# First chunk: x ahead of the weights, TensorE transposes and zero matmuls; last chunk: products grouped by tile

## The chip, the cores and the metric

The kernel runs on one core of a Trainium2 chip. The metric is the device time of one execution in microseconds (us). The profile's span is about 4 us shorter than the time of the same execution (2132.2 against 2136.0 for the traced run of the kernel before), so spans are compared with spans and times with times.

## The reference, cut to what matters

A Conformer block on x of shape (2, 4000, 512) in bfloat16:

```python
h = _layernorm(x); h = _silu(h @ w_ff1_a) @ w_ff1_b; x1 = x + 0.5 * h      # first feed-forward
h = _layernorm(x1); q, k, v = h @ w_q, h @ w_k, h @ w_v                     # attention over 4000 tokens
x2 = x1 + softmax(q k^T * scale) v @ w_o
...                                            # gated convolution with a batch norm over all tokens -> x3
h = _layernorm(x3); h = _silu(h @ w_ff2_a) @ w_ff2_b; x4 = x3 + 0.5 * h     # second feed-forward
return _layernorm(x4)
```

The change touches only the first 500 of the 8000 tokens in the first feed-forward and the last 500 in the second one.

## The kernel before

The tokens go in 16 chunks of 500, four tiles of 125 each. A helper records every instruction and its buffers and emits the waits, so nearly all matmuls have one source line. The start of the program, the feed-forward and the last layer norm (cuts marked):

```python
def load_x(self, c):
    if c == 0:
        for ti in range(TPC):       # four loads of 125 rows
            self.load(self.XT[ti], self.x_flat[ti * TILE:(ti + 1) * TILE, :], [self.bx[ti]])
    ...
# program
self.load_x(0)                      # sync queue
for k in range(self.NWA):           # 16 weight loads, ACT queue
    self.load_wa(i["w_ff1_a"], k, "ACT")
    self.load_wb(i["w_ff1_b"], 2 * k, 2 * k + 2, "ACT")
self.load_x(1)
...
for ti in range(TPC):               # first chunk: normalise, then transpose by DMA
    self.ln_norm(0, 0, ti, self.ltm[ti][0:TILE, :], self.b_ltm[ti], "DVE")
    self.transpose(self.lnT[0][:, ti], self.ltm[ti], [self.b_ltm[ti]], [self.b_lnT[0][ti]])

def weights():                      # emitted at the ninth step of the first chunk
    for n, name in (("q", "w_q"), ("k", "w_k"), ("v", "w_v")):
        self.transpose(self.wst[n][0], i[name], [], [self.wst[n][1]])
    self.load(self.wst["o"][0], ...w_o...)
    self.after(6, self.fold_weights)   # products w_q w_k^T ("M") and w_v w_o, amid the first chunk

def ff_chunk(self, c, old, hook, done):
    for f in range(FC):             # 16 blocks: 4 matmuls, Silu on ACT; some steps later 4 more, one per tile
        ...
        def second(f=f, s=s):
            for ti in range(TPC):
                self.mm(self.Yb[ti][0:TILE, :], self.P[s][:, ti * TILE:(ti + 1) * TILE], self.Wb[:, f, :], ...)
            if f == FC - 1:
                for ti in range(TPC):
                    self.residual(...)
                done()              # layer norm of all four tiles together, then the stores

# out_job: in the last chunk each tile is stored by itself
ev = self.S.dma("SP", k, lambda e: e.dma_start(dst[:, lo:ti + 1, :], self.osb[o][:, lo:ti + 1, :]),
                reads=self.b_osb[o][lo:ti + 1], writes=[self.b_out[c]])   # one record for all four
```

Of the kernel before, what the change touches and what calls it, by code (L numbers as in the profile page):

```python
# [52 lines left out]
class Sync:  # L53
# [105 lines left out]
    def dma(self, e, dkey, fn, reads=(), writes=()):  # L159
        req = self._required(reads, writes)  # L160
        prev = self.count[dkey]
        if prev > 0:
            v = req.get(dkey)
            if v is None or v.val < prev:
                req[dkey] = Ev(dkey, prev, {})
        self._emit_waits(e, req)
        ins = fn(self.eng[e])
        self.count[dkey] += 16
        ins.then_inc(self.sem[dkey], 16)
        ev = Ev(dkey, self.count[dkey], dict(self.clock[e]))  # L170
        self._bind(ev, reads, writes)
        return ev
# [46 lines left out]
class Conformer:  # L219
    LN_SLOTS = 4  # L220
    NP = 8

# [12 lines left out]
    def memory(self):  # L235
# [69 lines left out]
        self.b_P = [C.buf("P", oP + s * 1024, 1000) for s in range(self.NP)]  # L305
        self.ahi = C.view(oHL, CHUNK)
# [39 lines left out]
        self.h2c = C.view(oQ1, TPC * D).rearrange("p (t d) -> p t d", t=TPC)  # L346

# [55 lines left out]
        self.b_out = [Buf("out%d" % c) for c in range(NCK)]  # L403
# [51 lines left out]

    def act(self, out, in_, func, reads, writes, **kw):
        return self.S.op("ACT", lambda e: e.activation(out, in_, func, **kw), reads=reads, writes=writes)  # L457

    def load(self, dst, src, writes, eng="SP", reads=()):
        k = self.S.dsems[self.nxt("ld", 12)]  # L460
        return self.S.dma(eng, k, lambda e: e.dma_start(dst, src), reads=reads, writes=writes)  # L461

    def transpose(self, dst, src, reads, writes):
        k = self.S.dsems[12 + self.nxt("tr", 16)]
        return self.S.dma("SP", k, lambda e: e.dma_start_transpose(dst, src), reads=reads, writes=writes)  # L465

# [4 lines left out]
    def load_x(self, c):  # L471
        if c == 0:
            for ti in range(TPC):
                self.load(self.XT[ti], self.x_flat[ti * TILE:(ti + 1) * TILE, :], [self.bx[ti]])
# [89 lines left out]

    def ff_chunk(self, c, old, hook, done):

        pops = {0: old // 2, 1: old - old // 2, 2: 0, 3: 0, 7: 2, 11: 2}
        for f in range(FC):
            ps, b_ps = self.sbank()
            s = self.nxt("P", self.NP)  # L570
            out = ps[:, 0:CHUNK].rearrange("p (t k) -> p t k", t=TPC)
            for cc in range(DC):
                self.mm(out, self.Wa[:, cc, f * 128:(f + 1) * 128], self.lnT[c % 2][:, :, cc, 0:TILE],
                        cc == 0, cc == DC - 1, [self.b_Wa[f * self.NWA // FC]] + self.b_lnT[c % 2], b_ps)
            self.act(self.P[s], ps[:, 0:CHUNK], AF.Silu, [b_ps], [self.b_P[s]])

            def second(f=f, s=s):
                for ti in range(TPC):
                    self.mm(self.Yb[ti][0:TILE, :], self.P[s][:, ti * TILE:(ti + 1) * TILE],
                            self.Wb[:, f, :], f == 0, f == FC - 1, [self.b_Wb[f], self.b_P[s]],  # L580
                            self.b_Y[ti], inc=f == FC - 1 or ti == TPC - 1)
# [8 lines left out]
            self.tick()  # L590

# [271 lines left out]
    def out_job(self, c, at, gap=1):  # L863
        sl = self.nxt("ln", self.LN_SLOTS)
        o = c % 3
        last = c == NCK - 1
        t = at
        for ti in range(TPC):
            self.after(t, lambda ti=ti: self.ln_stats(c, sl, ti))
            if ti % 2:  # L870
                t += gap
        self.after(t, lambda: self.ln_aggr(c, sl))
        t += 2 * gap

        def tile(ti):
            self.ln_norm(c, sl, ti, self.osb[o][:, ti, :], self.b_osb[o][ti], "DVE")
            dst = self.out_flat[c * CHUNK:(c + 1) * CHUNK, :].rearrange("(t p) d -> p t d", p=TILE)
            lo = ti if last else 0
            if last or ti == TPC - 1:
                k = self.S.dsems[28 + self.nxt("od", 8)]  # L880
                ev = self.S.dma("SP", k, lambda e: e.dma_start(dst[:, lo:ti + 1, :], self.osb[o][:, lo:ti + 1, :]),
                                reads=self.b_osb[o][lo:ti + 1], writes=[self.b_out[c]])
                self.out_evs.append(ev)

        for ti in range(TPC):
            self.after(t, lambda ti=ti: tile(ti))
            if ti % 2:
                t += gap
# [33 lines left out]
    def constants(self):  # L922
        S = self.S
        S.op("POOL", lambda e: e.memset(self.neghalf, -0.5), writes=[self.b_neghalf])
        for j in range(TPC):
            S.op("DVE", lambda e, j=j: e.memset(self.ltm[j], 0.0), writes=[self.b_ltm[j]])
        S.op("POOL", lambda e: e.memset(self.ident, 0.0), writes=[self.b_ident])
# [8 lines left out]
        S.op("POOL", lambda e: e.memset(self.onef, 1.0), writes=[self.b_onef])  # L936
# [8 lines left out]
    def program(self, any_score):  # L945
# [7 lines left out]
        for k in range(self.NWA):  # L953
            self.load_wa(i["w_ff1_a"], k, "ACT")
            self.load_wb(i["w_ff1_b"], 2 * k, 2 * k + 2, "ACT")
        self.load_x(1)
        if not any_score:
            self.constants()

        for ti in range(TPC):  # L960
# [3 lines left out]
        for ti in range(TPC):  # L964
            self.ln_norm(0, 0, ti, self.ltm[ti][0:TILE, :], self.b_ltm[ti], "DVE")
            self.transpose(self.lnT[0][:, ti], self.ltm[ti], [self.b_ltm[ti]], [self.b_lnT[0][ti]])
# [112 lines left out]
        def ff2(c, old):  # L1079
# [10 lines left out]
            self.ff_chunk(c, old, hook, lambda: self.out_job(c, 5 if c < NCK - 1 else 0, 1 if c < NCK - 1 else 0))  # L1090

        for c in range(NCK):
            ff2(c, len(self.lags) if c else 0)
        self.drain()
# [56 lines left out]
```

## Time and profile before

| what | value | from |
|---|---|---|
| time | 2134.14 us median of 3 (2133.32 to 2136.76) | runs |
| span of the traced run | 2132.2 us | page |
| TensorE busy | 2058.9 us, 97% | page |
| first real matmul | 28.79 us | timeline |
| second weight product (w_v w_o) starts | 56.55 us | timeline |
| last matmul to the end | 17.6 us | timeline |

A digit in a row of slices is a busy share in tenths; "<-" in a timeline or a table of waits names what ended the wait. PE is TensorE, DVE the vector engine, ACT the scalar engine, POOL GpSimd, SP the sync engine; SPq and ACTq are the queues in which SP and ACT issue DMA transfers. PSUM is the memory into which TensorE writes. The second weight product is listed as a mark: everything after it keeps its order, so the time at which it starts tells what a change to the start is worth. In the trace before:

```profile
56.55 1.03 PE L453 MATMUL s<-keys 128*128 128x512 bf16 x4
```

### The profile page before, as it was taken

To read this page: it belongs to the slowest core of one execution; us is meant where nothing else is said; L and a number is where in the kernel's file an instruction comes from. 1 tells how busy PE (TensorE), PEld (TensorE's weight loads), DVE (VectorE), ACT (ScalarE), POOL (GpSimd) and SP (SyncE) were. 2 spreads that over 40 slices of the span, in tenths; PEclk is the share of its full clock that TensorE was granted. 3 is DMA by queue.
4 is the path that set the end of the run, shared out by engine and by line. 5 is a ranking of instruction groups with operands and counts; after the bars stand their busy time and mean duration, and the time that the engine had idled before them with its cause. 6 is when DMAs were issued, how large, how long until landed. Compare 5 with 4: busy or idle time off the path is not lost.

```text
span 2132.2 us, 24365 instructions
## 1 busy us (share of the span) xinstructions
PE 2058.9 (97%) x9674; PEld 1038.7 (49%) x9674; DVE 1090.5 (51%) x2229; ACT 732.7 (34%) x1248; POOL 122.9 (6%) x257
## 2 busy tenths in 40 slices
PE   4999999999999999999999999999987999999996
PEld 2555555554444444444444444444444555555553
DVE  2444433335555666656665666566745434444442
ACT  1433333333333333333333333333324433443332
POOL 0111100000000000000000000000000000000000
PEclk9999999999999999999999999999999999999998
DMA  7122222110000000004300000000233011111110
GB/s 177 34 56 59 59 60 59 49 49 11 11 5 13 18 15 20 8 18 114 80 10 18 15 18 13 15 18 16 59 107 99 21 38 35 35 30 40 40 38 23
DMA packets 199327, 85.39 MB, mean 40 GB/s; under 512 B 147873, under 2 KB 198692, under 8 KB 199204
## 3 DMA queue, kind: packets, MB, share of 16 engines
q1 hardware_dynamic: 186468, 75.35, 14.6%
q10 hardware_dynamic: 12736, 8.39, 1.5%
q8 instruction: 78, 1.28, 0.3%
q14 instruction: 45, 0.37, 0.1%
HBM read 29.53 MB, written 19.04 MB: 23 GB/s over the span
## 4 chain that ended last, share of the span: by engine, by line
PE 93%; DVE 3%; issue 1%; DMA 1%; ACT 0%; SPq 0%; POOL 0%; ACTq 0%; POOLq 0%; DVEq 0%
PE s L453 53%; PE y L453 39%; DVE work L711 1%; DVE work L716 1%; DVE work L673 0%; DMA xt<-in_x_dram 0%; ACT work L457 0%; DVE work L491 0%; SPq L465 0%; DMA work<-work 0%; DVE work L715 0%; DVE work L514 0%; POOL work L501 0%; DVE xt L560 0%; ACTq L461 0%
## 5 line engine op out<-in xcount | busy, mean ns | idle before, releaser
L457 ACT ACTIVATE work<-s 128x500 bf16<-128x500 f32 (+1 forms) x1068 | 626.8, 587 | 1266.6 <-PE s L453 1262.0
L453 PE MATMUL s<-work,wff 128*128 128x500 bf16 x2560 | 634.3, 378 | 32.2 <-DMA work<-work 28.8
L453 PE MATMUL y<-work,keys 128*128 128x500 bf16 x2048 | 519.1, 374 | 1.3
L453 PE MATMUL s<-work,keys 128*128 128x500 bf16 x2048 | 517.5, 374 | 0.1
L453 PE MATMUL y<-wff,work 128*125 128x512 bf16 x2048 | 514.8, 379 | 0.0
L673 DVE TENSOR_TENSOR work<-work 128x500 f32<-128x500 f32 x496 | 334.8, 675 | 304.6 <-ACT work L457 302.9
L453 PEld LDWEIGHTS s<-work,wff 128*128 128x128 bf16 x2560 | 251.1, 98 | 313.3 <-issue 33.7
L453 PEld LDWEIGHTS y<-wff,work 128*125 128x125 bf16 x2048 | 279.6, 137 | 176.4
L453 PEld LDWEIGHTS y<-work,keys 128*128 128x128 bf16 x2048 | 198.0, 97 | 244.4 <-DVE work L711 15.6
L453 PEld LDWEIGHTS s<-work,keys 128*128 128x128 bf16 x2048 | 199.2, 98 | 228.9 <-DVE work L602 0.6
L560 DVE SCALAR_TENSOR_TENSOR xt<-y,xt 125x512 bf16<-125x512 f32 x128 | 79.4, 683 | 385.5 <-PE y L453 385.5
L491 DVE BATCH_NORM_STATS2 work<-xt 125x6 f32<-125x512 bf16 x320 | 201.6, 679 | 16.8 <-DMA xt<-in_x_dram 16.8
L453 PE MATMUL s<-work 128*125 128x512 bf16 (+2 forms) x646 | 144.8, 347 | 20.8 <-DVE work L716 7.9
L501 POOL TENSOR_TENSOR work<-work 125x4 f32<-125x4 f32 x80 | 85.5, 1068 | 1189.2 <-DVE work L499 1189.2
L514 DVE TENSOR_SCALAR work<-xt,work 125x512 bf16<-125x512 bf16 x288 | 116.0, 449 | 20.1 <-POOL work L501 20.1
L453 PEld LDWEIGHTS s<-work 128*125 128x125 bf16 (+1 forms) x646 | 81.1, 139 | 72.1 <-issue 10.8
L560 DVE SCALAR_TENSOR_TENSOR xt<-s,xt 125x512 bf16<-125x512 f32 x64 | 43.8, 691 | 134.4 <-PE s L453 134.4
L755 DVE SCALAR_TENSOR_TENSOR wff<-wff,s 128x500 bf16<-128x500 f32 x64 | 43.2, 676 | 63.7 <-PE s L453 63.7
L457 ACT ACTIVATE wff<-s 128x500 f32<-128x500 f32 x64 | 37.6, 587 | 81.3 <-PE s L453 76.8
L560 DVE SCALAR_TENSOR_TENSOR xt<-s,work,xt 125x512 bf16<-125x512 f32 x64 | 48.0, 750 | 34.0 <-PE s L453 33.1
L453 PE MATMUL s<-keys,work 128*128 128x500 bf16 x256 | 64.4, 376 | 0.0
L457 ACT ACTIVATE work<-keys,work 128x500 bf16<-128x500 bf16 x64 | 49.6, 794 | 5.9 <-DMA wff<-in_w_ff_a_dram 4.0
(51 smaller groups left out, 397.7 us busy)
## 6 DMA issues: line engine op xcount, KB each, us to landing
xt<-in_x_dram SPq DMA_DIRECT2D x15, 500.0 KB
out_dram<-work SPq DMA_DIRECT2D x15, 500.0 KB
dcvd<-wff SPq DMA_DIRECT2D x52, 125.0 KB, 1.7
keys<-dcvd SPq DMA_DIRECT2D x13, 500.0 KB
wff<-in_w_ff_a_dram ACTq DMA_DIRECT2D x16, 256.0 KB
keys<-work SPq DMA_DIRECT2D x8, 512.0 KB, 3.5
keys<-keys SPq DMA_DIRECT2D x32, 128.0 KB
work<-work SPq DMA_TRANSPOSE x192, 2.5
```

The lines of the kernel that those rows point to most:

```text
L453: self.S.op("PE", lambda e: e.matmul(out, lhsT, rhs, start=start, stop=stop), reads=reads, writes=[bank], inc=stop if inc is None else inc)
L457: return self.S.op("ACT", lambda e: e.activation(out, in_, func, **kw), reads=reads, writes=writes)
L491: self.S.op("DVE", lambda e: e.bn_stats(self.st[sl][:, ti, :], self.XT[g]), reads=[self.bx[g]], writes=[self.b_st[sl][ti]])
L501: S.op("POOL", lambda e: e.tensor_tensor(out=self.rs[sl], in0=self.va[sl], in1=self.neghalf[0:TILE, :], op=ALU.pow), reads=[self.b_va[sl], ...
L514: self.S.op("DVE", lambda e: e.tensor_scalar(out, self.XT[g], self.mv[sl][:, ti, 0:1], self.rs[sl][:, ti:ti + 1], ALU.subtract, ALU.mult), ...
L560: self.S.op("DVE", lambda e: e.scalar_tensor_tensor(out=self.XT[g], in0=ps, scalar=scalar, in1=self.XT[g], op0=ALU.mult, op1=ALU.add), rea ...
L673: S.op("DVE", lambda e, p=p: e.tensor_tensor(out=self.acc[s], in0=self.acc[s], in1=self.P[p], op=ALU.add), reads=[self.b_P[p], self.b_acc[ ...
L711: S.op("DVE", lambda e, dc=dc: e.tensor_copy(self.OT[:, dc, :], self.Yb[dc][:, 0:CHUNK]), reads=[self.b_Y[dc]], writes=[self.b_OT[dc]])
L716: S.op("DVE", lambda e: e.tensor_tensor(out=self.alo, in0=self.acc[s], in1=self.ahi, op=ALU.subtract), reads=[self.b_acc[s], self.b_ahi], ...
L755: self.S.op("DVE", lambda e: e.scalar_tensor_tensor(out=self.G[gs][:, jj, 1:1 + CHUNK], in0=self.th[k], scalar=1.0, in1=ps[:, 0:CHUNK], op ...
```

## The change

The intent is to shorten the two stretches in which TensorE has nothing to do. At the start, x goes ahead of the weights in one queue, split into 80 and 45 rows; the first chunk is transposed on TensorE instead of by DMA; 20 matmuls on zeros run while it waits, to raise the clock. In the last chunk all first products come first, then the second products tile by tile, so that layer norm and store of a tile run beside the next tile's matmuls. Not in the cut below: a Silu of one column at the start, which makes ACT load its function table early, and 16 semaphores in turn for loads instead of 12. Core of the diff:

```diff
+    ROWS = ((0, 80), (80, TILE))
+    def warm(self, n):                     # n matmuls of the identity with zeros into a spare PSUM bank
+        ...
+    def transpose_pe(self, ti, s, eng):    # 4 TensorE transposes into PSUM, one copy on ACT or DVE
+        ...
     def load_x(self, c):
         if c == 0:
-            for ti in range(TPC):
-                self.load(self.XT[ti], ...)
+            self.load_rows(self.XTc[0], src, self.bx[0:TPC])
...
         for k in range(self.NWA):
-            self.load_wa(i["w_ff1_a"], k, "ACT")
-            self.load_wb(i["w_ff1_b"], 2 * k, 2 * k + 2, "ACT")
-        self.load_x(1)
+            self.load_wa(i["w_ff1_a"], k)
+            self.load_wb(i["w_ff1_b"], 2 * k, 2 * k + 2)
+            if k == 3:
+                self.load_x(1)
...
+        self.warm(20)
...
-            self.transpose(self.lnT[0][:, ti], self.ltm[ti], [self.b_ltm[ti]], [self.b_lnT[0][ti]])
+        for ti in range(TPC):
+            self.transpose_pe(ti, 0, ("ACT", "DVE")[ti % 2])
...
+    def ff_last(self, c, old):
+        for f in range(FC):
+            ... self.ff_first(c, f, *blocks[f])
+        for ti in range(TPC):
+            for f in range(FC):
+                self.ff_second(f, ti, *blocks[f], f == FC - 1)
+            ... residual, statistics, norm of this tile
+            self.store_out(c, self.osb[0], self.b_osb[0], ti, ti + 1, ("SP", "ACT"))   # writes=[Buf("out")]: a fresh record
```

More of the change, by code (lines that the diff above doesn't have):

```diff
@@ L157, in op, with dma @@
         return None
-    def dma(self, e, dkey, fn, reads=(), writes=()):
+    def dma(self, e, dkey, *fns, reads=(), writes=()):
         req = self._required(reads, writes)
@@ L166, in dma @@
         self._emit_waits(e, req)
-        ins = fn(self.eng[e])
-        self.count[dkey] += 16
-        ins.then_inc(self.sem[dkey], 16)
+        for fn in fns:
+            fn(self.eng[e]).then_inc(self.sem[dkey], 16)
+            self.count[dkey] += 16
         ev = Ev(dkey, self.count[dkey], dict(self.clock[e]))
@@ L305, in memory @@
         self.b_P = [C.buf("P", oP + s * 1024, 1000) for s in range(self.NP)]
+        self.zero, self.b_zero = self.P[0], self.b_P[0]
         self.ahi = C.view(oHL, CHUNK)
@@ L346, in memory @@
         self.h2c = C.view(oQ1, TPC * D).rearrange("p (t d) -> p t d", t=TPC)
+        self.late = [A.view(k * 1024, CHUNK) for k in range(FC - self.NP)]
+        self.b_late = [A.buf("late", k * 1024, 1000) for k in range(FC - self.NP)]
         ns = self.LN_SLOTS
@@ L402, in memory @@
         self.b_Y = [Buf("y%d" % i, excl=True) for i in range(4)]
-        self.b_out = [Buf("out%d" % c) for c in range(NCK)]
         self.keys2 = nc.dram_tensor("keys2", [TB * 128, D], BF16, kind="Internal").ap()
@@ L454, in mm @@
                   reads=reads, writes=[bank], inc=stop if inc is None else inc)
+    def warm(self, n):
+        ps, b_ps = self.sbank()
+        for k in range(n):
+            self.mm(ps[:, 0:CHUNK], self.ident, self.zero, True, True, [self.b_ident, self.b_zero], b_ps,
+                    inc=k == n - 1)
+    def transpose_pe(self, ti, s, eng):
+        ps, b_ps = self.sbank()
+        out = ps[:, 0:DC * 64].bitcast(BF16).rearrange("p (c k) -> p c k", c=DC)
+        for cc in range(DC):
+            self.S.op("PE", lambda e, cc=cc: e.transpose(
+                out[:, cc, 0:TILE], self.ltm[ti][0:TILE, cc * 128:(cc + 1) * 128], self.ident[0:TILE, 0:TILE]),
+                reads=[self.b_ltm[ti], self.b_ident], writes=[b_ps], inc=cc == DC - 1)
+        dst, src = self.lnT[s][:, ti, :, 0:TILE], out[:, :, 0:TILE]
+        if eng == "ACT":
+            self.act(dst, src, AF.Copy, [b_ps], [self.b_lnT[s][ti]])
+        else:
+            self.S.op("DVE", lambda e: e.tensor_copy(dst, src), reads=[b_ps], writes=[self.b_lnT[s][ti]])
     def act(self, out, in_, func, reads, writes, **kw):
@@ L459, in load, with load_rows @@
     def load(self, dst, src, writes, eng="SP", reads=()):
-        k = self.S.dsems[self.nxt("ld", 12)]
+        k = self.S.dsems[self.nxt("ld", 16)]
         return self.S.dma(eng, k, lambda e: e.dma_start(dst, src), reads=reads, writes=writes)
     def transpose(self, dst, src, reads, writes):
-        k = self.S.dsems[12 + self.nxt("tr", 16)]
+        k = self.S.dsems[16 + self.nxt("tr", 12)]
         return self.S.dma("SP", k, lambda e: e.dma_start_transpose(dst, src), reads=reads, writes=writes)
+    def load_rows(self, dst, src, writes):
+        k = self.S.dsems[self.nxt("ld", 16)]
+        return self.S.dma("SP", k, *[lambda e, lo=lo, hi=hi: e.dma_start(dst[lo:hi], src[lo:hi])
+                                     for lo, hi in self.ROWS], writes=writes)
     def store(self, dst, src, reads, writes):
@@ L472, in load_x @@
         if c == 0:
-            for ti in range(TPC):
-                self.load(self.XT[ti], self.x_flat[ti * TILE:(ti + 1) * TILE, :], [self.bx[ti]])
+            src = self.x_flat[0:CHUNK, :].rearrange("(t p) d -> p t d", p=TILE)
+            self.load_rows(self.XTc[0], src, self.bx[0:TPC])
         elif c < NCK:
@@ L562, in residual, with ff_first, ff_second @@
             reads=[b_ps, self.bx[g]] + list(b_scalar), writes=[self.bx[g]])
+    def ff_first(self, c, f, p, b_p):
+        ps, b_ps = self.sbank()
+        out = ps[:, 0:CHUNK].rearrange("p (t k) -> p t k", t=TPC)
+        for cc in range(DC):
+            self.mm(out, self.Wa[:, cc, f * 128:(f + 1) * 128], self.lnT[c % 2][:, :, cc, 0:TILE],
+                    cc == 0, cc == DC - 1, [self.b_Wa[f * self.NWA // FC]] + self.b_lnT[c % 2], b_ps)
+        self.act(p, ps[:, 0:CHUNK], AF.Silu, [b_ps], [b_p])
+    def ff_second(self, f, ti, p, b_p, inc):
+        self.mm(self.Yb[ti][0:TILE, :], p[:, ti * TILE:(ti + 1) * TILE], self.Wb[:, f, :],
+                f == 0, f == FC - 1, [self.b_Wb[f], b_p], self.b_Y[ti], inc=inc)
     def ff_chunk(self, c, old, hook, done):
@@ L568, in ff_chunk @@
         for f in range(FC):
-            ps, b_ps = self.sbank()
             s = self.nxt("P", self.NP)
-            out = ps[:, 0:CHUNK].rearrange("p (t k) -> p t k", t=TPC)
-            for cc in range(DC):
-                self.mm(out, self.Wa[:, cc, f * 128:(f + 1) * 128], self.lnT[c % 2][:, :, cc, 0:TILE],
-                        cc == 0, cc == DC - 1, [self.b_Wa[f * self.NWA // FC]] + self.b_lnT[c % 2], b_ps)
-            self.act(self.P[s], ps[:, 0:CHUNK], AF.Silu, [b_ps], [self.b_P[s]])
+            self.ff_first(c, f, self.P[s], self.b_P[s])
             def second(f=f, s=s):
                 for ti in range(TPC):
-                    self.mm(self.Yb[ti][0:TILE, :], self.P[s][:, ti * TILE:(ti + 1) * TILE],
-                            self.Wb[:, f, :], f == 0, f == FC - 1, [self.b_Wb[f], self.b_P[s]],
-                            self.b_Y[ti], inc=f == FC - 1 or ti == TPC - 1)
+                    self.ff_second(f, ti, self.P[s], self.b_P[s], f == FC - 1 or ti == TPC - 1)
                 if f == FC - 1:
@@ L590, in ff_chunk, with store_out @@
             self.tick()
+    def ff_last(self, c, old):
+        S, late = self.S, FC - self.NP
+        blocks = []
+        for f in range(FC):
+            if f < late:
+                blocks.append((self.late[f], self.b_late[f]))
+            else:
+                s = self.nxt("P", self.NP)
+                blocks.append((self.P[s], self.b_P[s]))
+            self.ff_first(c, f, *blocks[f])
+            self.pop({0: old // 2, 1: old - old // 2}.get(f, 0))
+            self.tick()
+        while self.later:
+            self.tick()
+        sl = self.nxt("ln", self.LN_SLOTS)
+        for ti in range(TPC):
+            for f in range(FC):
+                self.ff_second(f, ti, *blocks[f], f == FC - 1)
+            self.residual(self.Yb[ti][0:TILE, :], self.b_Y[ti], c * TPC + ti, 0.5)
+            self.ln_stats(c, sl, ti)
+            S.op("DVE", lambda e: e.bn_aggr(self.mv[sl][:, ti, :], self.st[sl][:, ti, :]),
+                 reads=[self.b_st[sl][ti]], writes=[self.b_mv[sl][ti]])
+            S.op("DVE", lambda e: e.tensor_scalar(self.va[sl][:, ti:ti + 1], self.mv[sl][:, ti, 1:2], EPS, None, ALU.add),
+                 reads=[self.b_mv[sl][ti]], writes=[self.b_va[sl]])
+            S.op("POOL", lambda e: e.tensor_tensor(out=self.rs[sl][:, ti:ti + 1], in0=self.va[sl][:, ti:ti + 1],
+                                                   in1=self.neghalf[0:TILE, ti:ti + 1], op=ALU.pow),
+                 reads=[self.b_va[sl], self.b_neghalf], writes=[self.b_rs[sl]])
+            self.ln_norm(c, sl, ti, self.osb[0][:, ti, :], self.b_osb[0][ti], "DVE")
+            self.store_out(c, self.osb[0], self.b_osb[0], ti, ti + 1, ("SP", "ACT"))
+    def store_out(self, c, o, b_o, lo, hi, engs=("SP",)):
+        dst = self.out_flat[c * CHUNK:(c + 1) * CHUNK, :].rearrange("(t p) d -> p t d", p=TILE)
+        rows = self.ROWS if len(engs) > 1 else ((0, TILE),)
+        for (r0, r1), eng in zip(rows, engs):
+            k = self.S.dsems[28 + self.nxt("od", 8)]
+            self.out_evs.append(self.S.dma(
+                eng, k, lambda e: e.dma_start(dst[r0:r1, lo:hi, :], o[r0:r1, lo:hi, :]),
+                reads=b_o[lo:hi], writes=[Buf("out")]))
     def q_group(self, b, qc, dc):
@@ L860, in pw2, with out_job @@
         self.residual(ps[0:TILE, :], b_ps, t * TPC + ti, 1.0)
-    def out_job(self, c, at, gap=1):
+    def out_job(self, c, at):
         sl = self.nxt("ln", self.LN_SLOTS)
         o = c % 3
-        last = c == NCK - 1
-        t = at
         for ti in range(TPC):
-            self.after(t, lambda ti=ti: self.ln_stats(c, sl, ti))
-            if ti % 2:
-                t += gap
-        self.after(t, lambda: self.ln_aggr(c, sl))
-        t += 2 * gap
+            self.after(at + ti // 2, lambda ti=ti: self.ln_stats(c, sl, ti))
+        self.after(at + 2, lambda: self.ln_aggr(c, sl))
         def tile(ti):
             self.ln_norm(c, sl, ti, self.osb[o][:, ti, :], self.b_osb[o][ti], "DVE")
-            dst = self.out_flat[c * CHUNK:(c + 1) * CHUNK, :].rearrange("(t p) d -> p t d", p=TILE)
-            lo = ti if last else 0
-            if last or ti == TPC - 1:
-                k = self.S.dsems[28 + self.nxt("od", 8)]
-                ev = self.S.dma("SP", k, lambda e: e.dma_start(dst[:, lo:ti + 1, :], self.osb[o][:, lo:ti + 1, :]),
-                                reads=self.b_osb[o][lo:ti + 1], writes=[self.b_out[c]])
-                self.out_evs.append(ev)
+            if ti == TPC - 1:
+                self.store_out(c, self.osb[o], self.b_osb[o], 0, TPC)
         for ti in range(TPC):
-            self.after(t, lambda ti=ti: tile(ti))
-            if ti % 2:
-                t += gap
+            self.after(at + 4 + ti // 2, lambda ti=ti: tile(ti))
     def fold_weights(self):
@@ L924, in constants @@
         S.op("POOL", lambda e: e.memset(self.neghalf, -0.5), writes=[self.b_neghalf])
+        S.op("DVE", lambda e: e.memset(self.zero, 0.0), writes=[self.b_zero])
         for j in range(TPC):
             S.op("DVE", lambda e, j=j: e.memset(self.ltm[j], 0.0), writes=[self.b_ltm[j]])
+        S.op("POOL", lambda e: e.memset(self.onef, 1.0), writes=[self.b_onef])
         S.op("POOL", lambda e: e.memset(self.ident, 0.0), writes=[self.b_ident])
@@ L935, in constants @@
             base=TILE - 1, channel_multiplier=-1), reads=[self.b_onec], writes=[self.b_onec])
-        S.op("POOL", lambda e: e.memset(self.onef, 1.0), writes=[self.b_onef])
         S.op("POOL", lambda e: e.memset(self.one3, 0.0), writes=[self.b_one3])
@@ L953, in program @@
         for k in range(self.NWA):
-            self.load_wa(i["w_ff1_a"], k, "ACT")
-            self.load_wb(i["w_ff1_b"], 2 * k, 2 * k + 2, "ACT")
-        self.load_x(1)
+            self.load_wa(i["w_ff1_a"], k)
+            self.load_wb(i["w_ff1_b"], 2 * k, 2 * k + 2)
+            if k == 3:
+                self.load_x(1)
         if not any_score:
             self.constants()
+        self.act(self.nr1, self.onef, AF.Silu, [self.b_onef], [self.b_nr1])
+        self.warm(20)
         for ti in range(TPC):
@@ L1088, in hook @@
                     self.ln_job(c + 1, 1, "in")
-            self.ff_chunk(c, old, hook, lambda: self.out_job(c, 5 if c < NCK - 1 else 0, 1 if c < NCK - 1 else 0))
-        for c in range(NCK):
+            self.ff_chunk(c, old, hook, lambda: self.out_job(c, 5))
+        for c in range(NCK - 1):
             ff2(c, len(self.lags) if c else 0)
+        self.ff_last(NCK - 1, len(self.lags))
         self.drain()
```

## The prediction

> **What bounds the kernel now.** I read the page first, from the busy shares to the slices to the chain, to find out whether anything but TensorE matters.
>
> ```profile
> PE 2058.9 (97%) x9674; PEld 1038.7 (49%) x9674; DVE 1090.5 (51%) x2229; ACT 732.7 (34%) x1248; POOL 122.9 (6%) x257
> PE   4999999999999999999999999999987999999996
> PEclk9999999999999999999999999999999999999998
> PE 93%; DVE 3%; issue 1%; DMA 1%; ACT 0%; SPq 0%; POOL 0%; ACTq 0%; POOLq 0%; DVEq 0%
> ```
>
> TensorE is busy 97% of 2132.2 us and carries 93% of the chain. Its row of slices is full but for the first, the last and two near the middle of the second half, so only about 73 us (2132.2 - 2058.9) of the span is not matmul. Next I read who TensorE waits for.
>
> ```profile
> PE s L453 <- DMA work<-work: 28.8, 1, 28.8
> PE s L453 <- ACT work L457: 7.9, 1, 7.9
> ```
>
> One wait of 28.8 us is the start: no matmul runs before the first chunk's transposed layer norm has arrived. The 7.9 us belongs to the start of the last feed-forward, around 1614 us, which the change does not touch. The chain at the start says what the 28.8 us consists of (start, length, what).
>
> ```profile
> 1.96 9.78 DMA xt<-in_x_dram
> ...
> 14.10 1.39 DVE work L514 x4
> ...
> 15.49 2.87 SPq L465
> ...
> 23.10 5.44 DMA work<-work
> 28.54 0.24 issue
> 28.79 7.34 PE s L453 x20
> 36.13 0.86 PE y L453 x4
> ```
>
> The last tile of x lands at 11.74 because it shares the DMA engines with 4.2 MB of weights; then layer norm; then from 15.49 to 28.54 four DMA transposes, issued one after the other. The first 20 matmuls take 7.34 us, 367 ns each, while later ones take 0.86 / 4 = 215 ns: the clock is low at first. At the end of the span the timeline shows:
>
> ```profile
> 2111.81 2.75 PE L453 MATMUL y<-wff,work 128*125 128x512 bf16 x12
> 2113.95 2.48 DVE L560 SCALAR_TENSOR_TENSOR xt<-y,xt 125x512 bf16<-125x512 f32 x4 [17.78 <-PE y L453]
> 2116.35 2.46 DVE L491 BATCH_NORM_STATS2 work<-xt 125x6 f32<-125x512 bf16 x4
> ...
> 2119.38 1.01 POOL L501 TENSOR_TENSOR work<-work 125x4 f32<-125x4 f32 x1 [24.70 <-DVE work L499]
> 2120.50 1.38 DVE L514 TENSOR_SCALAR work<-xt,work 125x512 bf16<-125x512 bf16 x4 [1.20 <-POOL work L501]
> ```
>
> The last matmul ends at 2111.81 + 2.75 = 2114.56. The 17.6 us to the end of the span are layer norm of all four tiles in batches (to 2121.9) and then the stores. The last store is issued at 2129.5, the first can't be before the first norm ends at 2120.91: three steps of about 2.85 us. In the code all four write one buffer record, so each waits for the one before to land.
>
> **What the Trainium skill says.** "TensorE: Matmul & The Clock Gate", Part 1, puts the array at 1.2 GHz when idle and at 2.4 GHz after a busy window of about 3.4 us, the window running free; the trace agrees on the factor of about two: 0.42 us between the first weight loads, 0.215 us later. After the last matmul the granted clock drops to 0.50 at about 2117, some 2.4 us later. (The clock column reads 1.00 at the start while matmuls run at half rate, so there I go by the durations.) "DMA: Bandwidth & Descriptors", in its section on why a DMA increments its semaphore by 16, says that a transfer runs on the largest number of engines up to 16 that divides its outermost dimension: 125 rows use 5 engines, 80 rows 16, 45 rows 15. The trace agrees: when only the next x chunk (125 rows) is left, 0.35 of 16 engines are busy, which is 5.6.
>
> ```profile
> 20.00:22.00 2.00, 0.00 (x0) 0.00 (x0) 0.00 (x0) 0.00 (x0) 0.00 (x0) 1.00 0.35 118
> ```
>
> (Columns: stretch, length, the five engines, clock, DMA share, GB/s.) The same page's "Issuing engines are not separate DMA queues" says that issuing from several engines saves sequencer time only; nothing here measures that yet. The clock page's Part 4 gives about 275 to 390 ns for a TensorE transpose and says that such transposes do not count as busy for the clock; this trace has none.
>
> **The change, part by part.** The instruction order of both builds shows differences in the first chunk and the last alone: 20 zero matmuls and 16 TensorE transposes ahead, and the last chunk's matmuls regrouped, the same in number.
>
> Start. x now goes first, over 16 and 15 engines, with the weights behind it in the same queue. Engine share: 512 KB / 16 = 32 KB. At the 118 GB/s / 5 = 23 GB/s per engine of the row above, that is 1.4 us after the first data at 1.96; with some 1 us to complete it lands at about 4.3 instead of 11.74. From first statistics to first norm took 28.74 - 24.58 = 4.16 us in the next chunk, where all four tiles were there: 8.5. Four norms take 1.38 us; transposes of a tile start as its norm ends, and the copies out of PSUM (ACT 0.59, DVE about 0.67 each, two per engine, DVE's after its norms) end about 2.8 us after the first norm began. The first real matmul is therefore at about 11.4 instead of 28.79: **17.4 us saved**. DMA transposes of this chunk disappear.
>
> Clock. Today 20 matmuls take 7.34 us against 20 x 0.2135 = 4.27: 3.1 us lost. The zero matmuls start when the identity is ready (about 1.8) and need at most 20 x 0.417 = 8.3 us, fewer once the clock rises; they end at about 7.7 to 10.1, and the gap to 11.4 is partly filled by transposes. I give one chance in three that the clock falls again in this gap, at about 2.5 us. **About 2.1 us saved.**
>
> Weights. 4.2 MB and the next x chunk (100 KB on each of 5 engines, 4.4 us there) now queue behind x. At some 20 GB/s per engine the eight pairs of 512 KB take about 1.8 us each, so the fifth pair lands at about 17 to 20; its matmuls are due at 11.4 + 11.1 = 22.5. No stall there. But the sync queue is held until some 20 us issuing them, and behind it stand x chunk 2, the next chunk's four transposes and those of w_q and w_k.
>
> ```profile
> 35.83 1.83 SPq L465 DMA_TRANSPOSE keys<-in_w_q_dram  x1
> 37.70 2.70 SPq L465 DMA_TRANSPOSE keys<-in_w_k_dram  x1
> ```
>
> Today w_k lands near 37.7 + 5.0 = 42.7, and the weight products that need it come after 104 matmuls, near 28.79 + 3.1 + 22.2 = 54.1: 11 us of slack. In the new kernel they are due at 11.4 + 22.2 = 33.6, 20 us earlier, while the queue gains only 6 to 10 us. I put a new stall of 0 to 5 us here: **1.5 us given back**.
>
> End. Sixty-four first-product matmuls, then 16 per tile: 16 x 0.2135 = 3.42 us per tile, in which DVE and POOL finish the tile before (0.69 + 0.62 + 0.15 + 0.17 + 1.0 + 0.41 and waits, 3.2 us). So only the last tile stands after the last matmul: 3.5 us with waits, then one store, split over both queues and 16 and 15 engines: 128-row stores of 125 KB took 1.7 us here, I take 2.2. 5.7 against 17.6: **11.9 us saved**.
>
> Sum: 17.4 + 2.1 - 1.5 + 11.9 = 29.9 us. 2134.1 - 29.9 = 2104.2; I shade it to 2105, as chains of small steps tend to have more waits than I count.
>
> **The rivals.** First, the wait moves rather than vanishes: the weight products stall on w_k or w_o by 5 to 7 us, or the second half of the first weights arrives late because x chunk 1 blocks five engines. For it: eleven us of slack against twenty us of earlier need. Against it: the DMA transposes of the first chunk, 13 us of that queue, are gone. It would give about 2110. Second, the clock falls back between zero matmuls and first real ones, as transposes may not keep it: +2 to 3 us, 2107. Third, the end is bound by DVE: if a tile takes longer than 3.42 us, delay accumulates, at most 1 to 2 us. Fourth, all hidden: it cannot be, since TensorE has nothing else to do in either stretch. Fifth, better than thought: x lands by 3.8 and no stall, 2101.
>
> **Range and chances.** The two ends, 28.8 + 3.1 + 17.6 = 49.5 us, are all that can be won; a gain of over 2% needs 42.7 us of them, with 11 us for x and layer norm and over 5 for the last tile still to be paid. So faster has 2%, slower 1%, the rest is within 2%. The range of 2100 to 2112 holds the rivals above.
>
> **What would show it.** First real matmul at 10.5 to 13.5 us; the first 20 real ones in 4.3 to 5 us (clock kept) or some 7 (lost); a wait of TensorE for w_k, w_v or w_o near 34 us, of 0 to 5 us; idle from the last matmul to the end of 5.5 to 6.5 us; nothing new in between. The prediction fails if the first chunk waits for weights by more than 6 us, or if x, in spite of being first, lands later than 6.

## The result, and the profile after

| | before | after |
|---|---|---|
| median time | 2133.73 us (2132.71 to 2136.76, 4 runs) | 2109.57 us (2107.03 to 2113.43, 4 runs) |
| span of the traced run | 2132.2 us | 2103.5 us |
| first real matmul | 28.79 | 12.44 |
| first 20 real matmuls take | 7.34 | 5.76 |
| second weight product starts | 56.55 | 41.67 |
| last matmul to the end | 17.6 | 5.4 |

The ratio is 0.9886, with a 95% interval from 0.9865 to 0.9907. Ratios are the mean time of one kernel's fast runs over that of the other's fast runs of the same rounds, so not quite the ratio of the medians quoted.

The page of the new kernel, to be held against the one in the prediction: TensorE's share is 98%, and the first and the last digit of its row have filled up, while the dip near the end of the third quarter stays.

```profile
PE 2063.4 (98%) x9708; PEld 1040.7 (49%) x9710; DVE 1092.4 (52%) x2235; ACT 733.8 (35%) x1251; POOL 124.0 (6%) x260
PE   8999999999999999999999999999987999999998
PE 94%; DVE 3%; SPq 1%; DMA 1%; ACT 1%; issue 0%; ACTq 0%; POOL 0%; POOLq 0%; DVEq 0%
```

The timeline of its start (start, length, engine, line, instruction; in brackets the idle time before and what ended it):

```profile
1.74 5.96 PE L458 MATMUL s<-work 128*128 128x500 bf16 x20 [1.74 <-DVE work L991]
5.89 2.47 DVE L522 BATCH_NORM_STATS2 work<-xt 125x6 f32<-125x512 bf16 x4 [3.60 <-DMA xt<-in_x_dram]
...
10.00 1.38 DVE L545 TENSOR_SCALAR work<-xt,work 125x512 bf16<-125x512 bf16 x4 [1.15 <-POOL work L532]
...
10.47 1.36 PE L473 MATMUL s<-work 125*128 125x125 bf16 x16 [2.77 <-DVE work L545]
...
12.44 5.76 PE L458 MATMUL s<-work,wff 128*128 128x500 bf16 x20 [0.61 <-DVE work L480]
...
24.06 5.25 SPq L491 DMA_TRANSPOSE work<-work  x4
...
29.34 2.57 SPq L491 DMA_TRANSPOSE keys<-in_w_q_dram  x1
...
31.95 1.81 SPq L491 DMA_TRANSPOSE keys<-in_w_k_dram  x1
...
33.81 3.20 SPq L491 DMA_TRANSPOSE keys<-in_w_v_dram  x1
...
37.05 0.58 SPq L487 DMA_DIRECT2D keys<-in_w_o_dram  x1
...
37.43 0.81 PE L458 MATMUL s<-keys 128*128 128x512 bf16 x3 [1.22 <-DMA keys<-in_w_k_dram]
...
41.67 1.02 PE L458 MATMUL s<-keys 128*128 128x512 bf16 x4 [1.72 <-DMA keys<-in_w_o_dram]
```

x is there at 5.89, all of it. The zero matmuls end at 7.70. The 16 TensorE transposes take 1.36 us together, and the first real matmul follows 0.61 us after them. Then two new waits: 1.22 us for w_k and 1.72 us for w_o, which sit in the sync queue behind the second chunk's transposes. The first 20 real matmuls still take 5.76 us, not 4.3. The windows of this stretch (length, then busy time of five engines, granted clock, DMA share, GB/s) say why:

```profile
10.00:12.00 2.00, 1.36 (x16) 0.89 (x16) 1.84 (x6) 1.04 (x2) 0.00 (x0) 0.95 0.87 253
12.00:14.00 2.00, 1.56 (x4) 0.59 (x5) 0.29 (x1) 0.14 (x1) 0.00 (x0) 0.50 0.84 226
14.00:16.00 2.00, 2.00 (x8) 0.82 (x7) 0.00 (x0) 0.90 (x2) 0.00 (x0) 0.69 0.67 187
```

The clock fell to half just before 12 us, some 4.2 us after the last zero matmul, although transposes ran from 10.47 to 11.83; the granted clock rose again between 14 and 16 us. The end of the span:

```profile
2096.19 1.89 PE L458 MATMUL y<-wff,work 128*125 128x512 bf16 x8
...
2098.12 0.69 DVE L591 SCALAR_TENSOR_TENSOR xt<-y,xt 125x512 bf16<-125x512 f32 x1 [0.56 <-PE y L458]
...
2100.60 0.41 DVE L545 TENSOR_SCALAR work<-xt,work 125x512 bf16<-125x512 bf16 x1 [0.66 <-POOL work L653]
```

DVE had been idle 0.56 us before the last tile, so the tiles' layer norms fit beside the matmuls. Only one tile's residual, layer norm (to 2101.01) and store (to 2103.5) stand after the last matmul at 2098.08.

### The profile page after: what moved, and what is told of

Read it like the earlier page. It is cut to its first block, busy times and chain, and to the rows that moved or that the text cites. A ratio compares the mean times of both kernels' runs of the same rounds, so it can differ in the third digit from the quotient of the medians.

```text
span 2103.5 us, 24444 instructions
## 1 busy us (share of the span) xinstructions
PE 2063.4 (98%) x9708; PEld 1040.7 (49%) x9710; DVE 1092.4 (52%) x2235; ACT 733.8 (35%) x1251; POOL 124.0 (6%) x260
## 4 chain that ended last, share of the span: by engine, by line
PE 94%; DVE 3%; SPq 1%; DMA 1%; ACT 1%; issue 0%; ACTq 0%; POOL 0%; POOLq 0%; DVEq 0%
PE s L458 54%; PE y L458 40%; DVE work L787 1%; SPq L491 1%; DVE work L792 1%; DMA xt<-in_x_dram 1%; DVE work L749 0%; ACT work L483 0%; DVE work L522 0%; DVE work L545 0%; DVE work L791 0%; ACTq L487 0%; SPq L487 0%; DMA keys<-in_w_o_dram 0%; POOL work L532 0%
## 5 line engine op out<-in xcount | busy, mean ns | idle before, releaser
L483 ACT ACTIVATE work<-s 128x500 bf16<-128x500 f32 (+2 forms) x1062 | 623.0, 587 | 1250.5 <-PE s L458 1240.4
L458 PE MATMUL y<-wff,work 128*125 128x512 bf16 x2016 | 506.6, 379 | 0.0
L458 PEld LDWEIGHTS y<-wff,work 128*125 128x125 bf16 x2016 | 275.2, 137 | 173.5
L458 PE MATMUL s<-work 128*125 128x512 bf16 (+3 forms) x666 | 150.2, 349 | 22.2 <-DVE work L792 7.9
L458 PEld LDWEIGHTS s<-work 128*125 128x125 bf16 (+2 forms) x666 | 82.8, 137 | 76.5 <-issue 12.2
```

Source lines behind the costliest of these rows:

```text
L458: self.S.op("PE", lambda e: e.matmul(out, lhsT, rhs, start=start, stop=stop), reads=reads, writes=[bank], inc=stop if inc is None else inc)
L483: return self.S.op("ACT", lambda e: e.activation(out, in_, func, **kw), reads=reads, writes=writes)
```

## The experiments

My theory after the traces of the two kernels was: the end wins what the traces say; the start wins less than its first matmul suggests, because w_o, behind the DMA transposes, now sets its pace; and the scatter of the new kernel comes from the clock. The rivals are named with each run.

### Repeat, and the two halves alone

The changed kernel again, without an edit.

> The changed kernel once more, to learn where its 6 us of scatter (2107 to 2113) comes from. Theory A (clock phase): [...]in some executions the clock stays low[...], at the start or after the 7.7 us wait near 1585 us; then longer runs show a lower mean granted clock (0.992 instead of 0.995) and spans some 4 to 6 us longer, and nothing else. Theory B (DMA): the weight products wait longer for w_k and w_o in some runs; then the clock would not differ. Median expected 2107 to 2112.

Measured: 2111.51 us median (2109.35 to 2113.4, 4 runs); before in the same rounds 2133.38 (9 runs). The traced run took 2109.84 with a span of 2106.0. Its timeline shows another course to the same place:

```profile
12.30 4.41 PE L458 MATMUL s<-work,wff 128*128 128x500 bf16 x20 [0.61 <-DVE work L480]
...
37.55 1.01 PE L458 MATMUL s<-keys 128*128 128x512 bf16 x3 [2.82 <-DMA keys<-in_w_k_dram]
42.17 1.02 PE L458 MATMUL s<-keys 128*128 128x512 bf16 x4 [0.42 <-DMA keys<-in_w_o_dram]
```

Here the clock was kept at first (4.41 us for 20), so TensorE came earlier to w_k and waited longer for it. In that wait the clock fell after all, as its windows show:

```profile
38.00:39.00 1.00, 1.00 (x4) 0.38 (x3) 0.00 (x0) 0.41 (x1) 0.00 (x0) 0.51 1.31 282
```

It reached the second weight product half a microsecond later than the first trace. Between these two traces the clock at the start thus made no difference at the mark. The rest of the 2.5 us between the two spans is in the wait before the second feed-forward: between 1540 and 1660 us, summing window length times (1 - granted clock) in windows of 2 us, the first trace lost 6.8 us and this one 8.5. Theory A holds for the scatter of these two traces, but in that later wait rather than at the start. The other runs, which left no trace, fit it: over all eight runs of the changed kernel the mean granted clock goes from 0.995 at the fastest (2107.03 and 2107.25 us) to 0.992 at the slowest (2113.43).

**The start alone**: the new start with the old last chunk (the old last-chunk code put back).

```diff
-        for c in range(NCK - 1):
-            ff2(c, len(self.lags) if c else 0)
-        self.ff_last(NCK - 1, len(self.lags))
+        for c in range(NCK):
+            ff2(c, len(self.lags) if c else 0)
```

> The changed start with the old last chunk. The traces say: first real matmul 28.79 to 12.44 (16.35 saved), 1.5 us of the 3.1 us of low clock saved, 2.9 us lost on w_k and w_o, so about 15.0 us in the span before the old end. Theory: 2133.7 - 15 = about 2118.5, and together with the tail alone the savings add up. Rival: the two parts interact (the new end depends on buffers or queues of the start), then the two savings differ from the whole by over 3 us.

Measured: 2121.19 us (2119.72 to 2121.66, 5 runs), 12.2 less than before, where 15 was expected. The second weight product starts at 40.91, 15.6 us earlier than in the trace before, but that trace is of a long execution: against the two other traces of the old start (55.25 in the end alone, 55.18 with free stores, both below) it is 14.3. The 2 us left to 12.2 are inside the interval of the ratio (0.9928 to 0.9955, some 3 us either way).

**The end alone**: the old start with the new last chunk (`ff_last` and what it calls put into the kernel before).

```diff
-        for c in range(NCK):
+        for c in range(NCK - 1):
             ff2(c, len(self.lags) if c else 0)
+        self.ff_last(NCK - 1, len(self.lags))
```

> The old start with the new last chunk. Traces: from the last matmul to the end 17.6 before, 5.4 after, so 12.2 us. Theory: 2133.7 - 12.2 = about 2121.5; first real matmul still at 28.8. Rival: grouping the matmuls by tile slows the last chunk itself; then the saving is less than 10.

Measured: 2121.88 us (2121.46 to 2124.03, 5 runs), 11.5 less than before. The last matmul ends at 2111.83 and the span at 2117.4, so 5.6 us instead of 17.6. The savings of the halves, 12.2 and 11.5, make 23.7; the whole made 21.9 in the same rounds and 24.2 in the first ones. They add up within the scatter. An interaction over 3 us isn't seen, but each of these ratios is known to some 3 us only, so the times don't exclude it; the traces speak against it, as each half shows its own gain alone (mark at 40.91, end at 5.6; in the whole 41.67 and 5.4).

**What the end consisted of**: the kernel before with one edit, a fresh buffer record for each store of the last chunk.

```diff
-                                reads=self.b_osb[o][lo:ti + 1], writes=[self.b_out[c]])
+                                reads=self.b_osb[o][lo:ti + 1], writes=[Buf("out")])
```

> The kernel before with one edit: the four stores of the last chunk no longer share one buffer record, so none waits for the landing of the one before; order of work, layer norm and 125-row stores stay. Theory: the last store is then issued at about 2122.2 instead of 2129.5, and the end comes 6 to 8 us earlier (2126 to 2128), more than half of what the new last chunk wins. Rival: the stores are slow because 125 rows run on five engines, so they queue there all the same and less than 3 us are won.

Measured: 2129.02 us (2128.2 to 2134.61, 4 runs), 4.4 less than before; in its trace 13.6 us from the last matmul to the end, 4.0 less than 17.6. The stores no longer wait for each other, as the sync queue's timeline shows, four issues in 1.73 us:

```profile
2123.58 1.73 SPq L881 DMA_DIRECT2D out_dram<-work  x4
```

The last is issued at 2125.3, but the span ends at 2130.8: 500 KB in stores of 125 rows take 5.5 us from there. I had expected 6 to 8 us from this edit; it is in between theory and rival. About a third of the 12 us that the end wins is the needless order of the stores; the other 8 are left for layer norm and stores beside the matmuls and for the store on more engines together; the split of the stores into 80 and 45 rows was not tried by itself.

### What sets the pace of the start

**No zero matmuls** (`self.warm(20)` taken out), and **34 instead of 20**:

```diff
-        self.warm(20)
+        self.warm(34)
```

> The changed kernel without its 20 zero matmuls. Both traces of the changed kernel pass the second weight product at the same time (41.7 and 42.2 us), though one kept the clock in the first real matmuls (4.4 us for 20) and the other lost it (5.8 us): there TensorE waits for w_o. Theory A: the queue of DMA transposes ahead of w_o sets the pace of the start, so the zero matmuls are worth nothing; the first 20 real ones take 6 to 7.5 us, the waits for w_k and w_o shrink by as much, the second weight product still starts at 41 to 42.5, and the time stays within 1 us of the changed kernel (about 2110). Rival B: the zero matmuls are worth the 1.5 to 3 us that the first 20 lose, and the time goes up by it (2112 to 2113).

> Thirty-four zero matmuls instead of 20, so that they last until the transposes. The first 20 real ones then take 4.3 to 4.5 us in every run. Theory A (w_o sets the pace): same time as the changed kernel, within 1 us, with longer waits for w_k and w_o. Rival B (the clock matters): 1.5 us faster.

Measured: without 2111.11 us (2106.91 to 2112.7, 4 runs), ratio to before 0.9877; with 34, 2111.07 us (2109.52 to 2112.81, 4 runs), ratio 0.9882. The changed kernel has 0.9886 and 0.9899. All three are the same. The trace without zero matmuls:

```profile
12.37 5.51 PE L458 MATMUL s<-work,wff 128*128 128x500 bf16 x20 [0.61 <-DVE work L480]
41.49 1.02 PE L458 MATMUL s<-keys 128*128 128x512 bf16 x4 [1.38 <-DMA keys<-in_w_o_dram]
```

With 34 they lasted until the transposes; the first real matmul came at 13.12 instead of 12.44, the next 20 took 4.41, and the second product started at 41.11. So the zero matmuls show no worth as long as w_o sets the pace. The times alone couldn't tell 1.5 us (their intervals are over 3 us either way); it is the marks that speak against it: 41.49 with none, 41.67 and 42.17 with 20, 41.11 with 34, where rival B asks for 1.5 to 3 us more without.

**w_q to w_o into the queue earlier**:

```diff
-            self.after(6, self.fold_weights)
+            self.after(14, self.fold_weights)
...
-                if c == 0 and f == 8:
+                if c == 0 and f == 0:
                     weights()
```

> The changed kernel with the loads of w_q, w_k, w_v and w_o put into the queue at the first step of the first chunk instead of the ninth, ahead of the second chunk's transposes; they then use the 4.5 us (19.5 to 24.1) in which the sync queue waits for the second chunk's layer norm. The matmuls stay in their order. Theory A: both waits (1.2 and 1.7, or 2.8 and 0.4) vanish, and 2.9 to 4 us are won: about 2107. Rival: the second chunk's transposes now land too late (they are needed at about 40 us), or the wait moves to them, and nothing is won.

Measured: 2104.93 us (2104.2 to 2107.21, 4 runs), ratio 0.9853 to before (median 2135.86 in these rounds). Both waits are gone, and no other has come in their place; the second product starts at

```profile
38.23 1.03 PE L458 MATMUL s<-keys 128*128 128x512 bf16 x4
```

3.4 us earlier. This version beats both kernels, by its medians. The changed kernel itself did not run in these rounds; its two variants above did, at 2111.1, some 6 us slower, about twice what the mark moved. Of the rest, 1.4 us stands in both their traces as a wait for transposes near 1577 us, which this trace does not have; what remains is not explained.

**Both edits**, 34 zero matmuls and early weights:

> Both edits. Theory A: with w_o out of the way the clock counts: 1 to 2 us faster than the early loads alone, about 2105 to 2106, so the effect of the zero matmuls, nil before, appears. Rival B: the two effects are independent, then the gain over the early loads alone is the same as the gain of 34 over 20 zero matmuls.

Measured: 2106.46 us (2106.14 to 2108.32, 4 runs), ratio 0.9864: not faster than the early loads alone, where 1 to 2 us were expected. The mark moves as expected, to 37.16, another 1.1 us; it isn't seen in the time, whose scatter is larger. The first real matmul came at 12.33, the first 20 took 4.41 against 5.77. What 14 more zero matmuls win once the wait is away is therefore 1.1 us at the mark, shown in one pair of traces only. It is not always there to be won: in the trace of the last experiment, with early weights and 20 zero matmuls, the first 20 took 4.41 too, and the mark is 36.94.

### The parts of the new start, one look each

These three ran once each; I read the traces. **x in one transfer of 125 rows**:

```diff
-            self.load_rows(self.XTc[0], src, self.bx[0:TPC])
+            self.load(self.XTc[0], src, self.bx[0:TPC])
```

> The changed kernel with x loaded in one transfer of 125 rows instead of 80 + 45. Theory (5 engines): 100 KB per engine instead of 32 at 23 GB/s, so x lands some 3 us later (first statistics at about 9 instead of 5.9) and the first real matmul at about 15.4 instead of 12.4; as w_o sets the pace, the second weight product starts within 1 us of 41.7 all the same. Rival: the split is worth nothing, statistics start within 0.5 us of 5.9.

Measured: statistics start at 9.18 instead of 5.89, first real matmul at 16.13 instead of 12.44. The 68 KB more per engine (100 - 32) in 3.3 us are 21 GB/s, near the 23 that I had taken, so the count of five engines fits. The second product starts at 44.65, three later and not within one: the transfers behind x in the queue are late too, w_o among them. There my theory was too narrow: w_o sets the pace, but x in front delays w_o.

**The first weights from the ACT queue again**:

```diff
-            self.load_wa(i["w_ff1_a"], k)
-            self.load_wb(i["w_ff1_b"], 2 * k, 2 * k + 2)
+            self.load_wa(i["w_ff1_a"], k, "ACT")
+            self.load_wb(i["w_ff1_b"], 2 * k, 2 * k + 2, "ACT")
```

> The changed kernel with the first weights issued from the ACT queue again, x alone on the sync queue. Theory: the 16 DMA engines are shared, so x lands later than 5.9 (the old kernel's last tile landed at 11.7, there on 5 engines; with 16 engines I expect 7 to 8), and copies on ACT wait behind the issues (ACT was held until 16.7 in the old kernel), so the first real matmul comes at about 17 to 18. On the other side the sync queue is free early, w_k and w_o land sooner. Rival: the queue makes no difference, first real matmul at 12.4.

Measured: statistics start at 6.83, about as expected, but the first real matmul only at 26.50, not 17 to 18:

```profile
22.09 1.83 ACTq L487 DMA_DIRECT2D wff<-in_w_ff_b_dram  x1
23.95 1.28 ACT L483 ACT_TABLE_LOAD   x1 [23.95 <-issue]
```

ACT issues the 16 loads until 23.9 and only then loads its table and copies its transposes out of PSUM. Why the issues hold ACT 7 us longer than in the kernel before (16.8) I did not find out. That the weights change queue is thus no detail: with copies on ACT, the issues may not stand there. x being first matters less (0.9 us here) than that.

**DMA transposes in the first chunk**:

```diff
-            self.transpose_pe(ti, 0, ("ACT", "DVE")[ti % 2])
+            self.transpose(self.lnT[0][:, ti], self.ltm[ti], [self.b_ltm[ti]], [self.b_lnT[0][ti]])
```

> The changed kernel with the first chunk's four transposes done by DMA as before, behind the weights in the sync queue. Theory: the transposes can only be issued when the queue is free, about 19.5, and take 10 us or so; first real matmul at 28 to 31, second weight product at about 54, time 2122 or more: the move to TensorE is the largest part of the start's gain. Rival: x first is the main gain, first real matmul at 20 or earlier.

Measured: first real matmul at 27.56, second product at 55.23, time 2127.6 in the one run. x is there at 5.68, yet only 1.2 us of the start are won: behind the weights in the queue, the transposes are late. They are issued from 20.90 on, though the first norm is done by 10.2. The rival falls. In this order of the queue the start's gain needs TensorE's transposes, and x ahead of the weights serves them; DMA transposes that don't stand behind the weights were not tried.

```profile
27.56 7.25 PE L458 MATMUL s<-work,wff 128*128 128x500 bf16 x20 [19.31 <-DMA work<-work]
```

### A wait elsewhere, since it makes the scatter

The clock is lost before the second feed-forward, where ACT issues that stage's weights while TensorE waits for ACT. The edit, on top of the early weights: those loads from the sync queue, and 12 zero matmuls in the wait.

```diff
+        self.warm(12)
...
         for k in range(clear, self.NWA):
-            self.load_wa(i["w_ff2_a"], k, "ACT")
+            self.load_wa(i["w_ff2_a"], k)
...
```

> Early w_q to w_o loads, and in addition the second feed-forward's weights issued from the sync queue instead of the ACT queue, with 12 zero matmuls ahead of the wait there. Theory: the 7.9 us for which TensorE waits for ACT near 1585 us shrink by the 4 us for which ACT is held by the issues, and the clock is lost for less time there (6.8 to 11.9 us of half clock now, 3.5 or less): 5 to 9 us faster than the early loads alone, about 2096 to 2100, and with less scatter. Rival: the wait is for the weights or for the batch norm itself, and moves: less than 2 us.

Measured: 2103.44 us (2101.05 to 2105.95, 5 runs), ratio 0.9853. The mechanism is there, but smaller than the list of waits says: TensorE waits 2.6 us for ACT instead of 7.9, but another 2.7 us of that stretch are the zero matmuls, which count as busy:

```profile
1585.29 2.69 PE L458 MATMUL s<-work 128*128 128x500 bf16 x12
...
1590.16 0.40 PE L458 MATMUL s<-work 128*125 128x512 bf16 x1 [2.18 <-ACT work L483]
```

The time without real matmuls is thus some 5.2 us instead of 7.9, where 4 us less were expected. The clock lost between 1540 and 1660 us is 3.4 us instead of 10.2 in the trace of the early loads. The span of the traced run is 2095.8. But the ratio is the same as that of the early loads alone. Part of the reason is that time and span differ by 5.6 us here (2101.41 against 2095.8; 5.5 to 5.8 in all five runs) and by 3.7 to 4.1 in the traced runs of the other kernels; what lies outside the span these runs do not show, so I leave it open and claim no gain. The two edits were not tried apart, and this run and that of the early loads are from different rounds.

## Why the prediction was right, step by step

It said 2105 with a range of 2100 to 2112; 2109.57 lies inside. The class, within 2%, was right as well. The stages, their waits and the stall were named rightly; the savings were summed too high, so that the point was 4.6 us too low, and the repeat's 2111.51 is only half a microsecond inside. What held the result in the range is its upper part, which had been kept for the first two rivals.

- **x first.** Predicted to land at 4.3, seen at 5.89. At 230 GB/s (window from 2 to 4 us) 512 KB take 2.2 us after the first data at about 2, and not the 1.4 that I worked out from 23 GB/s per engine; from there to the first statistics another 1.7 us pass, not 1. The 5.89 is 0.1 us short of the 6 us that the prediction had named as a sign of its failing. Direction and engine count held (x in 125 rows: 3.3 us later).
- **First real matmul.** Predicted at 11.4, seen at 12.44, which is the late x; the chain from statistics on took 6.55 us, predicted 7.1. The saving is 16.35, not 17.4.
- **Clock.** I gave one chance in three that it falls again in the gap. It fell in one trace (5.76 us for 20) and held in the other (4.41). The first 20 won 1.6 us in the first case and 2.9 in the second, but the term of 2.1 us was still wrong in kind: with w_o setting the pace, the clock here is worth nothing that shows (no zero matmuls: same time, same mark).
- **Weights behind the transposes.** The stall at the weight products was named, with its place and cause, and its size put at 1.5 us in a range of 0 to 5. It was 2.9 in one trace and 3.2 in the other. The step that was off: slack was worked out for w_k alone, and the queue was to gain 6 to 10 us. It gained 5.4 (w_o issued at 37.05 instead of 42.48) to 6.6, because it waited from 19.5 to 24.1 for the second chunk's layer norm; and w_o, which came last, had less slack than w_k (issued at 42.48, it needs 4.5 us to land in the trace after, and was due at 56.55: an estimate of 9.5 against 11). This is the term most undersized, and more so than its length says, because it also swallowed the clock's gain. Taking it away gave 3.4 us at the mark. The first rival, that the wait moves, is the half that came true.
- **End.** Predicted 11.9, seen 12.2 (5.4 against 17.6 in the traces; 11.5 in the times of the end alone).
- **Sum.** 29.9 predicted before the shading; 24.2 measured in the medians. At the mark the start won 14.9 and not 18.0 (17.4 + 2.1 - 1.5), which with the end makes 27.1 in the traces. Further, the trace from which I worked was of a long execution: 2136.0, where the median is 2133.7. Its first 20 matmuls took 7.34 us, while two traces of the same old start show 6.10 and 6.25. The loss of clock near 1600 us, 6.8 to 12.0 us over all traces but that of the run that edits this wait (3.4), adds a scatter of several us that no term of the sum had. I did not settle whether the new start makes that loss larger on the whole or the runs only happened to fall so.

The marks and the lost clock explain the spans of most traces of the new start and end. From the changed kernel (mark 41.67, lost clock 6.8, span 2103.5): the repeat has 0.5 + 1.7 more, so 2105.7, seen 2106.0; early weights have -3.4 + 3.4, so 2103.5, seen 2103.2; both edits have -4.5 + 3.4, so 2102.4, seen 2102.7; the variant with 34 zero matmuls has -0.6 + 3.4 and a wait of 1.4 us near 1577 us for transposes, so 2107.7, seen 2107.6. Two fit less well: without zero matmuls (-0.2 + 3.4 + 1.4) 2108.1, seen 2108.7; x in 125 rows (+3.0 + 0 + 1.3) 2107.8, seen 2108.9. This is an account, not a further experiment: in the lost clock each microsecond counts as if TensorE had work throughout.

## What to carry to other kernels

When the first matmul comes earlier, look for the next thing it will meet: every transfer that used to have slack is due earlier by the whole gain, and a queue that is issued in order hands the delay on. Put the load with the nearest date first, and keep DMA issues off an engine that something is waiting for. At the end of a kernel, arrange the work so that only one tile's chain stands behind the last matmul, and check that stores share no record that orders them for nothing; and judge gains of a few microseconds by marks in several traces, not by one trace of each kernel.

## What the Trainium skill lacked or had wrong

- "TensorE: Matmul & The Clock Gate", Part 1, asks for an idle window of about 3.4 us before the clock falls. Here 2.8 us of idle were enough once (the repeat's wait for w_k, granted clock 0.51 right after), and 2.4 us after the last matmul of the kernel before. The rule of no gaps over some 3 us, in the same page's "Why this matters for your kernels", is thus slightly too wide.
- The same page, Part 4, gives 275 to 390 ns for a TensorE transpose, and lacks what one costs in a row: the 16 of 125 x 128 took 1.36 us, 85 ns each, and 1.04 us (65 ns) right behind 34 zero matmuls. Its remark that transposes don't count as busy for the clock is not settled here. In the changed kernel's trace the clock fell 4.2 us after the last zero matmul, while they ran; but from the last zero matmul to the first real one it held over 3.9 us in the start alone (8.12 to 12.03) and 3.5 in the repeat, longer than the idle times above.
- "DMA: Bandwidth & Descriptors", "Issuing engines are not separate DMA queues", calls the sequencer's time for issuing usually small relative to the DMA itself. The 16 weight loads (4.2 MB) held ACT until 23.9 us when issued there beside x, and TensorE waited 13.6 us for a copy on ACT.
